# Scaled copies in three tiles, two relu groups on another engine, and a quad's work one stage later, in an attention and mixture-of-experts kernel

## The chip, the cores and the metric

The kernel runs on one core of one Trainium2 chip. The metric is the device time of one execution in microseconds; the median of the runs of a kernel is taken. The profile is one execution taken by the hardware profiler, with its own clock that begins at the first instruction; "at 162.98" means 162.98 us from there. The engines are TensorE (PE, with its weight loads PEld), VectorE (DVE), ScalarE (ACT), GpSimd (POOL) and SyncE (SP), which only issues DMAs.

## The reference

All values are fp32. A gated linear attention over batch 4, 8 heads, 768 tokens and head dimension 48 is followed by a mixture of 8 experts in which each of the 3072 tokens goes to one expert.

```python
f = 1 / (1 + exp(-f_logit))
for t in range(S):
    state = f[:, :, t, :, None] * state + einsum('bhd,bhe->bhde', k[:, :, t], v[:, :, t])
    y[:, :, t] = einsum('bhd,bhde->bhe', q[:, :, t], state)
x = y.transpose(0, 2, 1, 3).reshape(3072, 384)
logits = x @ w_gate                      # 8 experts
expert_idx = argmax(logits, 1)
gate_w = softmax(logits)[expert_idx]
for e in range(8):                       # rows of one expert
    h = maximum(x[rows_e] @ w1[e], 0)    # 384 x 1024
    out[rows_e] = gate_w * (h @ w2[e])   # 1024 x 384
```

## The kernel before

The first 140 us are the attention, in 12 units, and the routing: GpSimd scatters each token's row, with its token number and gate weight, to a table `xs` in HBM, sorted by expert. Nothing of the change touches this part.

Then the experts follow in order, 0 to 7. Each has three tiles of 128 rows (`TILES`), of which experts 0 and 1 have had their first tile done early. In experts 2 to 7 the first product (`widen_sums`, the matmuls of line 1310) is done with fewer multiplications, out of sums of the weights (`prepare_weights`, on GpSimd, line 1222, in place in the w1 tile and in `was`) and sums of the rows (`sum_rows`, on VectorE, line 1222, twelve per expert, in `xbs`). Its partial products are kept by ScalarE (line 1321) and joined by VectorE (line 1298), and ScalarE does the relu (line 1328). In experts 0 and 1 the first product is done directly (`widen`, line 387): its eight blocks of hidden units come in groups, and the relu of every other group is ScalarE's (line 397) and of the rest VectorE's (line 399).

The second product of two of the tiles is also done with fewer multiplications (`narrow_pair`, line 1360): seven products of quarter size. It needs `hidden_sums` (line 1416 and a difference), three sums of w2 (`weight_sums`, `wsum`: VectorE in experts 0 and 1, GpSimd from expert 2 on) and, in `narrow_pair` itself, two differences of the hidden units and one of w2's quarters. Four partial results are copied out of the accumulators by ScalarE, multiplied by the gate weight (`held`, line 1374); VectorE joins each with another product (`joined`, line 1378). The four copies lie in two tiles of two places each, `holdh0` and `holdh1`, handed out from the end of the list `places`: p1 and p4 in one, p5 and u2 in the other. The third tile's second product is `narrow_late` (line 403).

Rows beyond an expert's three tiles go to 8 slots of 32 rows, in two quads of four slots. A quad has its own rows (`quad_rows`: 16 small row loads and, for quad 1, four of token numbers), first weights (`quad_first`: four slots in two halves, 768 KB each, all in one tile `qw1` that both halves of both quads use in turn), second weights (`quad_second`: 1536 KB each, four buffers). `widen_quad` (line 1171) is half of a quad's first product, `turn_quad` (line 1188, "squares": `sq` in the tables) transposes its result for one slot, 32 by 32, and `turn` (`quad` in the tables) transposes its rows. Quad 0's second product rides along with the third tile of experts 4 to 7 (`narrow_riding`, line 1194); quad 1's is the last work of the kernel.

The order of the work is written out by hand. The instructions of each engine, SyncE's queue included, are issued in the order of the program. Within expert e there are three places at which loads are issued and quad products are made, numbered 3e, 3e + 1 and 3e + 2: `FIRST_AT`, `SECOND_AT`, `ROWS_AT` and `WIDE_AT` say which load or half product falls on which number. A half product falls at the start of the expert (3e) or after its `hidden_sums` (3e + 1), ahead of the loads of the same number; a load waits until the last reader of the buffer is done. `TASKS` says what VectorE does for the next expert, at four hooks of each expert: at its start, after its hidden sums, inside `narrow_pair` (`between`), and after it; `turn` transposes the next expert's rows, `sumN` makes N of its row sums. Sums not made there are made inside the next expert's `widen_sums`.

Between the first and second product of expert e the loads of expert e + 2 are issued: its rows (`load_expert`: four loads and up to three small ones), then its w1 (`load_first_weights`); its w2 (`load_second_weights`) follows the pair, since it takes the buffer of expert e's w2.

Of the kernel before, what the change touches and what calls it, by code (L numbers as in the profile page):

```python
# [11 lines left out]
F32 = mybir.dt.float32  # L12
# [37 lines left out]
SHORT = TILES * C - T  # L50
FIXED = np.array([SHORT if e in RIDE else TILES * C for e in range(E)])

ROWS_AT = {5: 0, 11: 1}
FIRST_AT = {
    4: [(0, 0, 0), (0, 1, 0)],
    7: [(0, 2, 0), (0, 3, 0)],
    9: [(0, 0, 1), (0, 1, 1)],
    10: [(0, 2, 1), (0, 3, 1)],
    13: [(1, 0, 0), (1, 1, 0)],
    14: [(1, 2, 0), (1, 3, 0)],  # L60
    16: [(1, 0, 1), (1, 1, 1)],
    17: [(1, 2, 1), (1, 3, 1)],
}
SECOND_AT = {8: [(0, 0)], 11: [(0, 1)], 14: [(0, 2)], 17: [(0, 3), (1, 0)], 19: [(1, 1)], 20: [(1, 2)]}
WIDE_AT = {9: (0, 0), 12: (0, 1), 16: (1, 0), 19: (1, 1)}


TASKS = {
    0: ("turn", "", "", ""),
    1: ("turn", "sum6", "", "sum4"),  # L70
    2: ("turn", "quad0 sum5", "sum6", "sum1"),
    3: ("turn", "sum6", "sum6", ""),
    4: ("sq00 turn", "sq01 sum3", "sum5", "sum4 quad1"),
    5: ("sq02 turn", "sq03 sum4", "sum6", "sum2"),
    6: ("turn", "sum6", "sum6", ""),
    7: ("sq10 sq11", "sq12", "sq13", ""),
}

# [93 lines left out]
def kernel(  # L172
# [205 lines left out]
    def widen(x, w, bank, blocks):  # L378

        rows = x["rows"]  # L380
        per = 512 // rows
        for b in blocks:
            i, f = divmod(b, per)
            if f == 0:
                x["h"] = bank(i)[:, 0 : per * rows].rearrange("p (f c) -> p f c", f=per)
            for j in range(KD):
                nc.tensor.matmul(  # L387
                    x["h"][:, f],
                    lhsT=w[0][:, j, b * 128 : b * 128 + 128],
                    rhs=x["xT"][:, j],  # L390
                    start=j == 0,
                    stop=j == KD - 1,
                )
            if f == per - 1:
                to = x["hT"][:, b - f : b + 1]
                if i % 2 == 0:
                    nc.scalar.activation(to, x["h"], AF.Relu)
                else:
                    nc.vector.tensor_scalar(to, x["h"], 0.0, None, op0=OP.max)
# [20 lines left out]
    HD = DM // 2  # L420
# [30 lines left out]
    def load_first_weights(e):  # L451
        w1t = wpool.tile([128, KD, F], F32, name="w1t")
        nc.sync.dma_start(w1t, moe_w1[e].rearrange(W1, p=128))
        weights[e] = [w1t]
# [6 lines left out]
    def slot(k, s, most):  # L461
        return nc.values_load(
            sloti[0:1, k, s : s + 1], [mybir.EngineType.SP], min_val=0, max_val=most
        )

    def load_expert(e):

        t = int(e < EARLY)
        x = load_rows(first[e] + t * C, int(FIXED[e]) - t * C)
        if e in RIDE:  # L470
            rows = xs[ds(slot(0, RIDE[e], NONE), T)]
            nc.sync.dma_start(x["tg"][C - T :, TILES - 1], rows[:, TOK:USED])
        return x
# [51 lines left out]
    with ExitStack() as st:  # L525
# [8 lines left out]
        for y in yt:  # L534
# [9 lines left out]
        held = {  # L544
            n: [ld.tile([128, SEG, C], F32, name=f"{n}{i}") for i in range(bufs)]
            for n, bufs in (("q", 4), ("k", 3), ("f", 2))
        }
# [581 lines left out]
    with ExitStack() as st:  # L1129
        bank, narrow_late, psz = tile_pools(st)  # L1130
        qp = st.enter_context(tc.tile_pool(name="qp", bufs=1))
# [80 lines left out]
        def minus(to, a, b, on=nc.vector):  # L1212
            on.tensor_tensor(to, a, b, op=OP.subtract)  # L1213
# [135 lines left out]
        def narrow_pair(x, s1, sums, between=lambda: None):  # L1349

            b, t1, t2, t4 = sums
            a = hidden_parts(x)
            one, two, both = (psz.tile([128, DM], F32, name="yps") for i in range(3))
            one, two, left, right = one[:, 0:HD], two[:, 0:HD], both[:, 0:HD], both[:, HD:DM]
            ysb = [ep.tile([128, DM], F32, name="ysb") for t in range(2)]
            gate = [x["tg"][:, t, 1:2] for t in range(2)]

            def product(to, h, w, start):
                for f in range(HB):
                    nc.tensor.matmul(  # L1360
                        to,
                        lhsT=h[:, f],
                        rhs=w[:, f],
                        start=start and f == 0,
                        stop=f == HB - 1,
                        skip_group_check=True,
                    )

            spare = [qp.tile([128, 2, HD], F32, name="held", tag=f"holdh{i}") for i in range(2)]
            places = [tile[:, i] for tile in spare for i in range(2)]  # L1370

            def held(part, t):
                to = places.pop()
                nc.scalar.mul(to, part, gate[t])  # L1374
                return to

            def joined(t, h, part, other):
                nc.vector.scalar_tensor_tensor(  # L1378
                    ysb[t][:, h * HD : h * HD + HD],
                    part,  # L1380
                    gate[t],
                    other,
                    op0=OP.mult,
                    op1=OP.add,
                )

            def leave(t):
                scatter(out, x["dst"][:, t : t + 1], ysb[t], N - 1, "out")

            product(one, a[0][0], b[0][0], True)  # L1390
            p1 = held(one, 0)
            minus(a[0][0], s1, a[0][0])
            product(left, a[0][1], b[1][0], True)
            minus(a[0][1], a[0][1], a[0][0])
            minus(b[0][1], b[1][1], b[0][1])
            product(right, a[1][1], t4, True)
            joined(0, 0, left, p1)
            between()
            p4 = held(right, 1)
            product(two, s1, t1, True)  # L1400
            p5 = held(two, 1)
            product(one, a[0][0], t2, False)
            u2 = held(one, 0)
            product(two, a[0][1], b[1][1], False)
            joined(0, 1, two, u2)
            leave(0)
            product(one, a[1][0], b[0][1], False)
            joined(1, 0, one, p4)
            joined(1, 1, one, p5)
            leave(1)  # L1410
# [20 lines left out]
        def fetch(at):  # L1431
            for piece in FIRST_AT.get(at, ()):
                quad_first(*piece)
            if at in ROWS_AT:
                quad_rows(ROWS_AT[at])
            for piece in SECOND_AT.get(at, ()):
                quad_second(*piece)

        for e in range(E):
            x, w = rows_of[e], weights[e]  # L1440
            end, wide = e == E - 1, e >= EARLY
# [18 lines left out]
            def wide_quad(at):  # L1460
                if at in WIDE_AT:
                    q, b = WIDE_AT[at]
                    widen_quad(quads[q], b)
# [18 lines left out]
                tasks(1)  # L1482
            wide_quad(3 * e + 1)
            if e + 2 < E:
                rows_of[e + 2] = load_expert(e + 2)
                load_first_weights(e + 2)
            fetch(3 * e + 1)
            if end:
                halves_of(quads[1], 0)
# [16 lines left out]
    with tc.If(todo > 0):  # L1506
# [80 lines left out]
        with ExitStack() as st:  # L1587
            bank, narrow_late, psz = tile_pools(st)
            hp = st.enter_context(tc.tile_pool(name="hp", bufs=1))
            with tc.For_i(0, E) as e:  # L1590
# [10 lines left out]
                with tc.For_i(e * REGION + skip, rows_to, C) as at:  # L1601
                    x = load_rows(at)
# [57 lines left out]
```

## Time and profile before

| | |
|---|---|
| median of 3 runs | 385.8 us (385.88, 385.8, 381.94) |
| the profiled execution | 381.89 us |
| its span, from the first to the last instruction | 380.0 us |
| TensorE's mean granted clock | 0.999 |
| busy: TensorE, VectorE, GpSimd, ScalarE | 361.1, 280.4, 223.1, 161.8 us |
| moved by DMA | 94.92 MB, 250 GB/s on the mean |

A row of the timeline gives the start in us, the duration, the engine ("SPq" is SyncE's queue: the time of the issue, not of the transfer), the line, the operation, the tile written and those read, and how many instructions were merged. Brackets hold the idle time of the engine just before and what ended it. A busy TensorE is not one at its peak, but an idle one does nothing.

### The profile page before, as it was taken

How to read it: one execution, taken by the hardware profiler on the slowest of the kernel's cores; microseconds unless marked ns; L12 is line 12 of the kernel's file. 1: busy time of each engine (PE TensorE's matmuls, PEld its weight loads, DVE VectorE, ACT ScalarE, POOL GpSimd, SP SyncE). 2: the span in 40 equal slices, each digit the busy share in tenths (PEclk: the TensorE clock that was granted, in tenths of full speed). 3: DMA queues.
4: the chain of work that ended last, by engine and by line, in shares of the span. 5: the costliest groups of instructions: out<-in, count | busy, mean ns of one | idle time of the engine just before them, and what ended most of it. 6: DMA issues, size and time to landing. Idle time of an engine off the chain costs nothing.

```text
span 380.0 us, 9175 instructions
## 1 busy us (share of the span) xinstructions
PE 361.1 (95%) x3438; PEld 310.5 (82%) x3438; DVE 280.4 (74%) x565; ACT 161.8 (43%) x326; POOL 223.1 (59%) x240
## 2 busy tenths in 40 slices
PE   8999999999999999998799799999998999999993
PEld 8889889888889678987797597977795599499692
DVE  6999989896974645569669848867977667878850
ACT  7899885875433001110353154245235125316410
POOL 5444255758954411069799399299579629946112
PEclk9999999999999999999999999999999999999999
DMA  7999765758994368999447699761999989981151
GB/s 261 392 384 367 255 235 201 246 197 277 401 364 134 123 178 269 288 352 299 149 152 213 218 376 262 291 218 19 258 348 383 217 329 365 373 301 41 22 187 47
DMA packets 56916, 94.92 MB, mean 250 GB/s; under 512 B 20968, under 2 KB 41003, under 8 KB 55840
## 3 DMA queue, kind: packets, MB, share of 16 engines
q1 hardware_dynamic: 53696, 84.62, 68.4%
q0 software_dynamic: 3168, 9.64, 6.7%
q8 instruction: 29, 0.48, 0.5%
q14 instruction: 23, 0.19, 0.2%
HBM read 79.23 MB, written 15.21 MB: 248 GB/s over the span
## 4 chain that ended last, share of the span: by engine, by line
PE 63%; DVE 16%; POOL 8%; issue 6%; ACT 2%; DMA 2%; SPq 1%; POOLq 0%; DVEq 0%
PE yps L1360 11%; PE hps L1310 9%; PE s L647 6%; PE yt L671 6%; PE xp L770 6%; DVE hT L1298 5%; PE yps L1194 4%; PE hps L387 4%; PE s L387 3%; POOL wsum L1213 3%; PE kp L660 3%; DVE xbs L1222 3%; PE yt L692 2%; POOL was L1222 2%; PE dp L708 2%
## 5 line engine op out<-in xcount | busy, mean ns | idle before, releaser
L246 POOL DMA_INDIRECT out_dram<-ysb,dst x26 | 26.4, 1017 | 89.0 <-DVE ysb L1378 50.7
L1360 PE MATMUL yps<-w2t,hT 128*128 128x192 f32 x256 | 45.3, 330 | 5.8 <-ACT held L1374 4.3
L1360 PEld LDWEIGHTS yps<-w2t,hT 128*128 128x128 f32 x256 | 41.6, 190 | 10.4 <-ACT held L1374 5.4
L1328 ACT ACTIVATE hT<-hT 128x352 f32<-128x352 f32 (+1 forms) x48 | 23.9, 506 | 39.1 <-DVE hT L1298 38.9
L1310 PE MATMUL hps<-xbs,w1t 128*128 128x176 f32 (+1 forms) x216 | 37.6, 318 | 0.2
L613 POOL TENSOR_TENSOR k<-k,r 128x1024 f32<-128x1024 f32 (+1 forms) x11 | 25.2, 2293 | 20.5 <-ACT r L609 14.6
L246 POOL DMA_INDIRECT xs<-xr,posi x24 | 27.3, 1135 | 16.2 <-issue 4.9
L1310 PEld LDWEIGHTS hps<-xbs,w1t 128*128 128x128 f32 x216 | 34.0, 190 | 0.7 <-issue 0.7
L1374 ACT ACTIVATE held<-yps,tg 128x192 f32<-128x192 f32 x32 | 12.4, 419 | 51.1 <-DVE ysb L1378 35.5
L653 DVE COPY_PREDICATED at<-mpack,s 128x512 f32<-128x512 uint8 x48 | 32.0, 729 | 1.9 <-PE s L647 1.9
L1321 ACT COPY hT<-hps 128x352 f32<-128x352 f32 (+1 forms) x54 | 24.8, 459 | 18.0 <-PE hps L1310 11.7
L1298 DVE TENSOR_TENSOR hT<-hps,hT 128x352 f32<-128x352 f32 (+1 forms) x42 | 22.3, 530 | 12.5 <-ACT hT L1321 5.9
L595 DVE TENSOR_TENSOR_SCAN sum<-g,cap 128x1032 f32<-128x1032 f32 (+1 forms) x14 | 29.4, 2104 | 2.1 <-ACT g L588 2.1
L1222 POOL TENSOR_TENSOR was<-w1t 128x256 f32<-128x256 f32 x30 | 26.1, 886 | 3.1 <-issue 2.6
L1194 PE MATMUL yps<-qw,hqT 128*32 128x192 f32 (+1 forms) x192 | 27.5, 381 | 0.2 <-issue 0.2
L647 PE MATMUL s<-q,k 64*128 64x128 f32 x384 | 26.8, 282 | 0.1
L1378 DVE SCALAR_TENSOR_TENSOR ysb<-yps,tg,held 128x192 f32<-128x192 f32 x32 | 12.6, 414 | 19.0 <-PE yps L1360 19.0
L647 PEld LDWEIGHTS s<-q,k 64*128 64x128 f32 x384 | 23.1, 187 | 2.9 <-issue 1.2
L770 PE MATMUL xp<-wx,ys 128*128 128x104 f32 x192 | 24.9, 279 | 0.4 <-issue 0.4
L1360 PE MATMUL yps<-wsum,hT 128*128 128x192 f32 x128 | 23.6, 327 | 1.2 <-DVE hT L1213 1.2
L671 PE MATMUL yt<-at,v 128*48 128x128 f32 x384 | 24.6, 276 | 0.1
L770 PEld LDWEIGHTS xp<-wx,ys 128*128 128x128 f32 x192 | 22.9, 192 | 1.2 <-issue 0.9
(157 smaller groups left out, 836.7 us busy)
## 6 DMA issues: line engine op xcount, KB each, us to landing
w1t<-in_moe_w_dram SPq DMA_DIRECT2D x8, 1536.0 KB
w2t<-in_moe_w_dram SPq DMA_DIRECT2D x8, 1536.0 KB, 12.5
qw<-in_moe_w_dram SPq DMA_DIRECT2D x16, 768.0 KB, 8.8
qw<-in_moe_w_dram SPq DMA_DIRECT2D x8, 1536.0 KB
k<-in_ku_dram SPq DMA_DIRECT2D x12, 512.0 KB
q<-in_qu_dram SPq DMA_DIRECT2D x12, 512.0 KB, 6.8
f<-in_fu_dram SPq DMA_DIRECT2D x10, 512.0 KB, 5.6
xs<-pad SPq DMA_DIRECT2D x8, 600.0 KB
```

Of the source, the lines that this page charges most:

```text
L246: ins = nc.gpsimd.indirect_dma_start(out=dst, out_offset=bass.IndirectOffsetOnAxis(ap=idx, axis=0), in_=src, in_offset=None, bounds_check= ...
L387: nc.tensor.matmul(x["h"][:, f], lhsT=w[0][:, j, b * 128 : b * 128 + 128], rhs=x["xT"][:, j], start=j == 0, stop=j == KD - 1,)
L595: nc.vector.tensor_tensor_scan(x["sum"][:, part].rearrange("p s c -> p (s c)"), x["g"][:, part].rearrange("p s c -> p (s c)"), cap[:, part ...
L647: done["score"] = nc.tensor.matmul(ps[h][:, p], lhsT=x["k"][r, s], rhs=x["q"][r, s], start=True, stop=True).ins
L653: nc.vector.copy_predicated(x["at"][:, a, h], _bc(causal, 1, HP), x["ps", a][h])
L671: nc.tensor.matmul(x["yt"][a][DP * (h ^ a) : DP * (h ^ a) + D, p], lhsT=x["v"][:, a, 2 * p + h], rhs=x["at"][:, a, h, p], start=p == 0, st ...
L770: nc.tensor.matmul(x["xp", a][:, p], lhsT=x["ys", a][:, p], rhs=wx[:, p, 0:XW] if a else wx[:, p, E:WX], start=True, stop=True,)
L1194: nc.tensor.matmul(yp[r], lhsT=h[:, f, at : at + T], rhs=w[:, f, cols], start=f == order[0], stop=f == order[-1], skip_group_check=True,)
L1222: on.tensor_tensor(to, first[1], second[1], op=op)
L1298: nc.vector.tensor_tensor(place(to), one, place(other), op=op)
L1310: nc.tensor.matmul(banks[n][:, g], lhsT=lhs[:, C * g : C * g + C], rhs=rhs, start=op == "new" and g == 0, stop=True, skip_group_check=True,)
L1360: nc.tensor.matmul(to, lhsT=h[:, f], rhs=w[:, f], start=start and f == 0, stop=f == HB - 1, skip_group_check=True,)
```

## The change

1. The four scaled copies of `narrow_pair` lie in three tiles: p1 in the first, p4 and u2 in the second, p5 in the third. The first join is issued ahead of the difference of w2's quarters instead of behind it.
2. In experts 0 and 1 all four relu groups are ScalarE's (`x["wide"]` is False there; the tiles done early have no such entry and stay as they were).
3. In expert 0 the w1 of expert 2 is loaded ahead of its rows instead of behind them. The other experts keep their order.
4. Quad 1 goes one stage on: its rows are loaded in expert 4 (14) instead of expert 3 (11), its first weights from 13 to 19 instead of 13 to 17, its half products are made at 19 and 21 instead of 16 and 19. Quad 0's second weights 3 are loaded at 16 instead of 17, quad 1's 1 at 17 instead of 19. Two of the squares and the turn of quad 1 go one hook or more on, and row sums move with them.

```diff
-ROWS_AT = {5: 0, 11: 1}
+ROWS_AT = {5: 0, 14: 1}
 FIRST_AT = {
...
-    13: [(1, 0, 0), (1, 1, 0)],
-    14: [(1, 2, 0), (1, 3, 0)],
-    16: [(1, 0, 1), (1, 1, 1)],
-    17: [(1, 2, 1), (1, 3, 1)],
+    13: [(1, 0, 0)],
+    14: [(1, 1, 0)],
+    16: [(1, 2, 0), (1, 3, 0)],
+    19: [(1, 0, 1), (1, 1, 1), (1, 2, 1), (1, 3, 1)],
 }
-SECOND_AT = {8: [(0, 0)], 11: [(0, 1)], 14: [(0, 2)], 17: [(0, 3), (1, 0)], 19: [(1, 1)], 20: [(1, 2)]}
-WIDE_AT = {9: (0, 0), 12: (0, 1), 16: (1, 0), 19: (1, 1)}
+SECOND_AT = {8: [(0, 0)], 11: [(0, 1)], 14: [(0, 2)], 16: [(0, 3)], 17: [(1, 0), (1, 1)], 20: [(1, 2)]}
+WIDE_AT = {9: (0, 0), 12: (0, 1), 19: (1, 0), 21: (1, 1)}
...
 TASKS = {
     0: ("turn", "", "", ""),
-    1: ("turn", "sum6", "", "sum4"),
-    2: ("turn", "quad0 sum5", "sum6", "sum1"),
+    1: ("turn", "sum6", "", "sum3"),
+    2: ("turn", "quad0 sum3", "sum6", "sum3"),
     3: ("turn", "sum6", "sum6", ""),
-    4: ("sq00 turn", "sq01 sum3", "sum5", "sum4 quad1"),
-    5: ("sq02 turn", "sq03 sum4", "sum6", "sum2"),
-    6: ("turn", "sum6", "sum6", ""),
+    4: ("sq00 turn", "sq01 sum3", "sum5", "sum4"),
+    5: ("turn", "sq02 sum3", "sum6 quad1", "sum3"),
+    6: ("turn", "sq03 sum3", "sum6", "sum3"),
     7: ("sq10 sq11", "sq12", "sq13", ""),
 }
...
-                if i % 2 == 0:
+                if i % 2 == 0 or x.get("wide") is False:
                     nc.scalar.activation(to, x["h"], AF.Relu)
                 else:
                     nc.vector.tensor_scalar(to, x["h"], 0.0, None, op0=OP.max)
...
-            spare = [qp.tile([128, 2, HD], F32, name="held", tag=f"holdh{i}") for i in range(2)]
-            places = [tile[:, i] for tile in spare for i in range(2)]
+            spare = [qp.tile([128, 2, HD], F32, name="held", tag=f"holdh{i}") for i in range(3)]
+            places = [spare[i][:, j] for i, j in ((1, 1), (2, 0), (1, 0), (0, 0))]
...
             minus(a[0][1], a[0][1], a[0][0])
-            minus(b[0][1], b[1][1], b[0][1])
             product(right, a[1][1], t4, True)
             joined(0, 0, left, p1)
+            minus(b[0][1], b[1][1], b[0][1])
             between()
...
             if e + 2 < E:
+                if e == 0:
+                    load_first_weights(e + 2)
                 rows_of[e + 2] = load_expert(e + 2)
-                load_first_weights(e + 2)
+                if e > 0:
+                    load_first_weights(e + 2)
```

## The prediction

> **What bounds the kernel now.** I read the page first, then TensorE in order of time from 143 us on (the only stretch that the change touches), then the idle times that end there, then the stretches of the DMA queue and the issues of SyncE's queue.
>
> ```profile
> span 380.0 us, 9175 instructions
> PE 361.1 (95%) x3438; PEld 310.5 (82%) x3438; DVE 280.4 (74%) x565; ACT 161.8 (43%) x326; POOL 223.1 (59%) x240
> ```
>
> TensorE is busy for 361.1 of 380.0 us, so everything that an edit without a matmul can bring lies in some 19 us of holes. No matmul is added or removed. The holes of the expert stage, by the timeline of TensorE (start, duration, engine, line, operation, tiles, count, and in brackets the idle time before it and what ended it):
>
> ```profile
> 176.10 0.92 PE L1360 MATMUL yps<-w2t,hT 128*128 128x192 f32 x4 [1.51 <-DVE hT L399]
> ...
> 183.21 2.87 PE L1360 MATMUL yps<-w2t,hT 128*128 128x192 f32 x16 [1.99 <-ACT held L1374]
> ...
> 210.87 1.54 PE L1360 MATMUL yps<-wsum,hT 128*128 128x192 f32 x8 [1.16 <-DVE hT L1213]
> 213.54 2.87 PE L1360 MATMUL yps<-w2t,hT 128*128 128x192 f32 x16 [1.13 <-ACT held L1374]
> ...
> 244.23 2.87 PE L1360 MATMUL yps<-w2t,hT 128*128 128x192 f32 x16 [0.25 <-ACT held L1374]
> ...
> 249.74 0.86 PE L1310 MATMUL hps<-xT,was 128*128 128x176 f32 x4
> ...
> 274.82 2.87 PE L1360 MATMUL yps<-w2t,hT 128*128 128x192 f32 x16 [0.88 <-ACT held L1374]
> 277.52 0.76 PE L1310 MATMUL hps<-xT,was 128*128 128x176 f32 x4
> ...
> 294.76 2.33 PE L1171 MATMUL hps<-qw,qxT 128*32 128x512 f32 x17 [1.03 <-DMA qw<-in_moe_w_dram]
> ...
> 311.82 0.76 PE L1310 MATMUL hps<-xT,was 128*128 128x176 f32 x4
> ...
> 324.13 2.78 PE L1171 MATMUL hps<-qw,qxT 128*32 128x512 f32 x24
> ...
> 341.21 0.76 PE L1310 MATMUL hps<-xT,was 128*128 128x176 f32 x4
> ```
>
> Experts 5, 6 and 7 begin at 277.52, 311.82 and 341.21. Expert 5 is the slow one: 34.3 us, with a quad's first product (L1171) in it that waits for its weights. Behind the `held` rows stands one line of the waits (engine and line, what it waited for, us in total, times, longest):
>
> ```profile
> ACT held L1374 <- DVE ysb L1378: 35.5, 8, 8.0
> ```
>
> In all 8 experts a scaled copy waits for a join on VectorE. The second copy p4 lies in the tile that holds p1, which the join reads: a write behind a read. The joins queue behind w2's sum.
>
> **The change, part by part.** Expert 1 first. VectorE's rows, then GpSimd's, SyncE's, a group of ScalarE, and two stretches of the DMA queue (busy times of the engines, clock, DMA share, GB/s):
>
> ```profile
> 162.98 1.76 DVE L370 STREAM_TRANSPOSE xT<-xrow 128x1152 f32<-128x1152 f32 x1
> ...
> 167.50 0.69 DVE L399 TENSOR_SCALAR hT<-hps 128x512 f32<-128x512 f32 x1 [2.71 <-PE hps L387]
> ...
> 176.15 1.11 DVE L1416 TENSOR_TENSOR hsum<-hT 128x512 f32<-128x512 f32 x1
> ...
> 178.50 1.03 DVE L1213 TENSOR_TENSOR hT<-hsum,hT 128x512 f32<-128x512 f32 x1
> ...
> 180.59 1.48 DVE L1213 TENSOR_TENSOR w2t<-w2t 128x768 f32<-128x768 f32 x1
> ```
> ```profile
> 166.90 0.72 POOL L1222 TENSOR_TENSOR was<-w1t 128x256 f32<-128x256 f32 x1 [2.59 <-issue]
> ...
> 183.29 0.72 POOL L1222 TENSOR_TENSOR w1t<-w1t,was 128x256 f32<-128x256 f32 x1
> ```
> ```profile
> 154.15 3.21 SPq L340 DMA_DIRECT2D xrow<-xs  x4
> ...
> 157.97 0.43 SPq L453 DMA_DIRECT2D w1t<-in_moe_w_dram  x1
> ```
> ```profile
> L397 ACT ACTIVATE hT<-hps 128x512 f32<-128x512 f32 x4 | 2.4, 599 | 23.9 <-PE hps L387 13.8 <-DMA xrow<-xs 10.1
> ```
> ```profile
> 157.00:161.00 4.00, 4.00 (x27) 4.00 (x26) 1.23 (x3) 1.15 (x3) 0.00 (x0) 1.00 1.26 232
> 161.00:164.50 3.50, 3.50 (x20) 3.22 (x20) 2.60 (x4) 0.00 (x0) 1.94 (x2) 1.00 1.00 397
> ```
>
> The relus: four of 0.69 us leave VectorE and cost ScalarE four of 0.60 us; ScalarE was idle for 23.9 us ahead of that group, which hides them. The 1.51 us hole goes. Late next is the hidden sum, which stands in VectorE's order behind the turn of expert 2's rows, w2's three sums and six row sums. Here the swap of the loads counts. The rows fill the queue over 157 to 161 us and w1 over 161 to 164.5; w1 ahead (1536 KB at 397 GB/s, 4.0 us) puts the rows' end at about 165. The turn began at 162.98, some 2 us behind the rows' end, so it goes to about 167, 4 us later. VectorE had 2.71 us of idle time and two relus (1.4 us) there, which the change frees, so the hidden sum starts at 176, as before. Bounds of the swap: 0 (the turn waits less than I think) to 4 us (all of it comes through). GpSimd's sums of expert 2's first weights can start some 2.5 us sooner than 166.90 and end at 181.5 instead of 184.0; without the swap they would end 0.4 us behind the start of expert 2 found below, so at this place the swap only keeps GpSimd off the path. On TensorE: `left` ends at 175.2 instead of 176.8, the product of s1 starts at 177.2, that of s1 minus a00 at 179.5 (as before: hsum, two differences of about 1.1 us). From there p4 and p5 no longer wait for a join: the 1.99 us go, but the last product needs w2's sum, which now runs behind the join, 181.0 to 182.5. Expert 2 starts at 183.6 instead of 185.9: **2.3 us** (1 to 3).
>
> Expert 2: two of five row sums move behind the pair.
>
> ```profile
> 208.22 1.57 DVE L1222 TENSOR_TENSOR xbs<-xT,xbs 128x192 f32<-128x192 f32 x2
> 209.71 0.41 DVE L1222 TENSOR_TENSOR xbs<-xbs,xT 128x192 f32<-128x192 f32 x1
> ```
>
> Half of 1.57 and 0.41 make 1.2 us, so the 1.16 hole closes, and 1.13 with the tiles: **2.2 us**. The sums are issued after the pair, in front of expert 3's turn, where VectorE has slack. Experts 3 and 4: **0.25 and 0.88**. Together TensorE reaches expert 5 about 5.6 us earlier, at **271.9**.
>
> Expert 5 loses the quad's first half (L1171, 2.7 us as at 324.13), the second quad's turn and one set of squares. What is left has the shape of expert 4 without its hole: 277.52 - 249.74 - 0.88 = 26.9 us. Expert 6 gets the first half in the place of the second; expert 7 gets the second half ahead of everything, 2.7 us more. The squares are VectorE's transposes:
>
> ```profile
> L1188 DVE STREAM_TRANSPOSE hqT<-hq 32x256 f32<-32x256 f32 x32 | 13.9, 436 | 3.1 <-ACT hq L1179 2.6
> ```
>
> A set is four of 436 ns, 1.7 us. Expert 6 gets one in exchange for three of six row sums, less than 1 us more ahead of its pair (bounds 0 and 1 us; I take 0). In expert 7 two sets, 3.5 us, must wait for the second half's product and relu; the joins behind them start about as long after the first matmul of the expert's own as before, since that comes 2.7 us later too (bounds 0 and 2 us, taken as 0). If no load is late, expert 6 starts at 298.8, expert 7 at 328.1, and the end is 328.1 + 2.7 + (380.0 - 341.2) = **369.6**.
>
> **The loads.** The second half's four loads now wait for the first half's product in expert 6 (one buffer), and stand behind w2 of expert 7 and three loads of second weights. Can the queue bring them by 328.1? Stretches of the queue, then SyncE's issues, then the traffic of its hardware queue from 312 to 341 us, and of all issues those of a quad's rows (two quads, KB each, us to landing):
>
> ```profile
> 247.00:266.00 19.00, 19.00 (x157) 14.33 (x160) 13.72 (x24) 9.21 (x21) 17.76 (x18) 1.00 0.42 118
> ...
> 312.00:340.00 28.00, 27.95 (x217) 22.38 (x217) 23.47 (x40) 11.43 (x26) 22.36 (x23) 1.00 1.02 356
> ```
> ```profile
> 247.17 0.40 SPq L458 DMA_DIRECT2D w2t<-in_moe_w_dram  x1
> ...
> 264.23 0.39 SPq L1149 DMA_DIRECT2D qw<-in_moe_w_dram  x1
> ...
> 273.44 0.35 SPq L453 DMA_DIRECT2D w1t<-in_moe_w_dram  x1
> ...
> 278.07 0.40 SPq L458 DMA_DIRECT2D w2t<-in_moe_w_dram  x1
> ...
> 301.28 0.35 SPq L453 DMA_DIRECT2D w1t<-in_moe_w_dram  x1
> ...
> 312.06 0.40 SPq L458 DMA_DIRECT2D w2t<-in_moe_w_dram  x1
> ```
> ```profile
> q1 hardware_dynamic: 6003, 9.44, 92.9%
> ```
> ```profile
> qrow<-xs SPq DMA_DIRECT2D x32, 12.0 KB, 1.9
> ```
>
> From 247.17 to 264.23 SyncE issues one w2 and then the quad's 20 small row loads, and the DMA engines are busy for 0.42 of it: 17 us in which the queue runs dry. The change moves that block behind w2 of expert 6, whose issue waits for expert 4's last product (278.07, 0.55 us behind 277.52). The chain from there: 271.9 + 0.55 for w2; 17.1 for the block and 2.3 more for the 768 KB load now ahead of it (0.79 MB at 28 us per 9.44 MB), so the third second-weight load is issued at 291.9; 9.2 to w1 of expert 7 (264.23 to 273.44, the same sequence), 301.1; 10.8 for w1 and two first-half loads (301.28 to 312.06, the same kinds), 311.9, which is about when expert 6's quad product wants them (298.8 + 12.1). Then w2, three second weights and the four loads: 4 x 1.573 + 4 x 0.786 MB = 9.44 MB, which is what the queue moved from 312 to 340 in before: 28 us. So they are in at 339.9; with 1 us of slack at either seam closed up, at 337.9. I take **338.9**. TensorE stands from 328.1 to 338.9, and the end is 338.9 + 2.7 + 38.8 = **380.4**. What was gained is handed back at the start of expert 7.
>
> On the rule: the Trainium skill, DMA: Bandwidth & Descriptors, section Issuing engines are not separate DMA queues, says that the sequencer's issue time is usually small relative to the DMA itself. Here 16 issues of 12 KB and four smaller ones take most of 17 us for 0.2 MB, and the trace disagrees. By that rule the block would cost its bytes alone, about 0.6 us, the chain would be some 15 us shorter, and the end would be that of the rival without a late load.
>
> **The rivals.**
>
> Nothing late: span 369.6. The loads must be in 11 us sooner than my chain has it. It holds if SyncE's block of small loads runs faster in its new place, or if the transfers behind it overlap more than one after the other. For it: the queue had room in before (0.42 over 247 to 266). Against it: the same bytes stood in the queue at a share of 1.02. Each us that my chain is too long is a us gained, so the cases between (373 to 377) belong here.
>
> Slower, through expert 1's queue on VectorE: if the turn of expert 2's rows ends not at 168.8 but 4 us later, w2's sums, the row sums and the hidden sum follow it in order, expert 2 starts at 187.6, and since the chain hangs on expert 4's end, everything is 4 us later: 384.4. It decides from a turn that begins later than 170.9. For it: the queue is full there (shares of 1.26 and 1.00), so w1 delays the rows by its whole length; against: that length is only 4.0 us, and VectorE's idle time takes up most of it.
>
> The change does not do what it says: p4's wait is for the shared accumulator of `left` and `right`, not for the tile. Then the four `held` holes stay (4.25 us); about 1 us of each goes with the earlier join, so 2 us come back, and the chain ends at 382.5.
>
> **How the numbers follow.** 1% (3.8 us) is about what a measurement of this kernel can tell. Forecast 0.48, with 377 to 384; nothing or little late 0.33 (369 to 377); slower through VectorE 0.14; not as said 0.05. The profiled execution took 381.89 us, 1.9 beyond its span; the timed runs were 385.88, 385.8 and 381.94, two levels 3.9 apart, and the profile is on the lower. My span 380.4 makes 382.3 on the lower level and 386.2 on the upper; I cannot say on which the next median falls and put down 384. The range goes from a mostly kept gain on the lower level (371.5 to 373) to 384.4 + 1.9 + 3.9 less a little: 373 to 389. The gains over 1% are 0.35 (nothing late and a small part of the forecast), slower 0.16.
>
> **What would show it.** The relu's 1.51 us and the `held` rows of 1.99, 1.13 and 0.88 gone; expert 5 starting near 272 and taking about 27 us; SyncE's small row loads now between about 275 and 291; four 768 KB loads issued near 315; and, decisive, an idle time of some 11 us on TensorE ahead of L1171 at the start of expert 7, ended by the DMA of `qw`. I am wrong if that idle time is under 5 us, or if the turn at expert 1 begins past 171.

## The result and the profile after

The changed kernel takes 386.69 us (median of 20 runs, 382.92 to 389.05), the kernel before 382.76 us in the same comparison (20 runs, 379.02 to 385.92). The ratio is 1.0107, with a 95% interval of 1.0077 to 1.0138: **1% slower**. The forecast was no change (a span of 380.4 us against 380.0). The profiled execution after has a span of 384.9 us, 4.9 more than before, so the traces show the difference with the same sign and about the same size.

The page of the changed kernel, its first lines:

```profile
span 384.9 us, 9171 instructions
PE 364.3 (95%) x3438; PEld 308.9 (80%) x3438; DVE 279.4 (73%) x561; ACT 164.3 (43%) x330; POOL 220.7 (57%) x240
```

TensorE has the same 3438 matmuls and is busy 3.2 us longer. That alone says that not all of the loss is waiting; some matmuls ran slower or alone. TensorE's timeline from expert 1 on (start, duration, line, tiles, count, and in brackets the idle time before it and what ended it):

```profile
178.47 1.57 PE L1360 MATMUL yps<-wsum,hsum 128*128 128x192 f32 x8 [2.24 <-DVE hsum L1416]
180.83 1.54 PE L1360 MATMUL yps<-wsum,hT 128*128 128x192 f32 x8 [0.79 <-DVE hT L1213]
182.63 2.87 PE L1360 MATMUL yps<-w2t,hT 128*128 128x192 f32 x16 [0.26 <-ACT held L1374]
185.33 0.81 PE L1310 MATMUL hps<-xT,was 128*128 128x192 f32 x4
...
195.74 1.54 PE L1310 MATMUL hps<-xbs,w1t 128*128 128x192 f32 x8 [0.50 <-DVE xbs L1222]
203.61 1.56 PE L403 MATMUL yps<-w2t,hT 128*128 128x384 f32 x4 [0.43 <-ACT hT L1328]
...
275.19 0.76 PE L1310 MATMUL hps<-xT,was 128*128 128x176 f32 x4
...
303.34 0.76 PE L1310 MATMUL hps<-xT,was 128*128 128x176 f32 x4
...
335.13 1.05 PE L1171 MATMUL hps<-qw,qxT 128*32 128x512 f32 x2 [0.94 <-DMA qw<-in_moe_w_dram]
337.17 1.05 PE L1171 MATMUL hps<-qw,qxT 128*32 128x512 f32 x2 [0.99 <-DMA qw<-in_moe_w_dram]
339.62 1.04 PE L1171 MATMUL hps<-qw,qxT 128*32 128x512 f32 x2 [1.41 <-DMA qw<-in_moe_w_dram]
342.10 4.10 PE L1171 MATMUL hps<-qw,qxT 128*32 128x512 f32 x18 [1.43 <-DMA qw<-in_moe_w_dram]
346.13 0.86 PE L1310 MATMUL hps<-xT,was 128*128 128x176 f32 x4
```

Read from the bottom. At the start of expert 7 four rows in a row wait for `qw`, the four loads of quad 1's second half. From 335.13 to 346.13 TensorE does 24 matmuls that took 2.78 us in expert 6 of before: 8.2 us lost. Expert 5 begins at 275.19, 2.3 us sooner than before (277.52), expert 6 at 303.34, 8.5 us sooner; 2.7 of these are the quad product that is only postponed to expert 7, so 5.8 were gained. Expert 6 up to its last product takes 31.8 us instead of 29.4 (303.34 to 335.13, with the first 0.94 of the wait; 311.82 to 341.21), and 5.8 - 2.4 - 8.2 makes 4.8 of the 4.9 us lost (the rest is rounding). In expert 1, the two old holes (1.51 and 1.99) have become three new ones (2.24, 0.79, 0.26): 3.50 us out, 3.29 us in.

SyncE's queue and the stretches of the DMA engines behind it (for the stretches: busy times of the engines, then granted TensorE clock, DMA share, GB/s):

```profile
275.43 0.39 SPq L458 DMA_DIRECT2D w2t<-in_moe_w_dram  x1
...
277.96 1.90 SPq L340 DMA_DIRECT2D qrow<-xs  x4
...
294.56 0.39 SPq L1149 DMA_DIRECT2D qw<-in_moe_w_dram  x1
...
302.25 0.35 SPq L453 DMA_DIRECT2D w1t<-in_moe_w_dram  x1
```
```profile
283.00:295.00 12.00, 11.96 (x106) 8.20 (x105) 10.21 (x16) 5.44 (x12) 11.52 (x15) 1.00 0.22 62
295.00:312.00 17.00, 15.55 (x97) 14.59 (x95) 14.59 (x30) 5.10 (x13) 10.46 (x10) 1.00 1.00 307
312.00:344.00 32.00, 26.86 (x190) 17.01 (x194) 19.47 (x38) 7.38 (x17) 23.04 (x24) 0.96 1.06 381
```

The rows of the quad stand between 277.96 and 294.56. From 283 to 295 the DMA engines are at a share of 0.22. Then they are full, 1.00 and 1.06, until the last late load is in. What they could have moved in those 12 us is missing at 335; e4 below tests this.

### The profile page after: what moved, and what is told of

The parts are those of the page before. It is cut to its first block, busy times and chain, and to the rows that moved or that the text cites. A ratio compares the mean times of both kernels' runs of the same rounds, so it can differ in the third digit from the quotient of the medians.

```text
span 384.9 us, 9171 instructions
## 1 busy us (share of the span) xinstructions
PE 364.3 (95%) x3438; PEld 308.9 (80%) x3438; DVE 279.4 (73%) x561; ACT 164.3 (43%) x330; POOL 220.7 (57%) x240
## 4 chain that ended last, share of the span: by engine, by line
PE 61%; DVE 18%; DMA 8%; SPq 5%; issue 3%; ACT 3%; POOL 1%; POOLq 0%; DVEq 0%
PE hps L1310 11%; PE yps L1360 8%; PE s L647 6%; PE yt L671 6%; DVE hT L1298 6%; PE xp L770 6%; PE yps L1194 4%; DMA qw<-in_moe_w_dram 4%; SPq L1149 3%; PE s L387 3%; DVE xbs L1222 3%; PE hps L387 3%; PE kp L660 3%; DMA xrow<-xs 3%; PE hps L1171 2%
## 5 line engine op out<-in xcount | busy, mean ns | idle before, releaser
L595 DVE TENSOR_TENSOR_SCAN sum<-g,cap 128x1032 f32<-128x1032 f32 (+1 forms) x14 | 29.3, 2102 | 2.0 <-ACT g L588 1.9
L1188 DVE STREAM_TRANSPOSE hqT<-hq 32x256 f32<-32x256 f32 x32 | 14.0, 436 | 14.2 <-ACT hq L1179 13.8
L1378 DVE SCALAR_TENSOR_TENSOR ysb<-yps,tg,held 128x192 f32<-128x192 f32 x32 | 12.6, 414 | 15.8 <-PE yps L1360 12.2
L1222 POOL TENSOR_TENSOR was<-w1t 128x256 f32<-128x256 f32 x30 | 23.2, 790 | 1.1 <-PE hps L387 0.6
```

The costliest lines, as they stand in the source:

```text
L595: nc.vector.tensor_tensor_scan(x["sum"][:, part].rearrange("p s c -> p (s c)"), x["g"][:, part].rearrange("p s c -> p (s c)"), cap[:, part ...
L1222: on.tensor_tensor(to, first[1], second[1], op=op)
```

## The experiments

Time is given as a ratio to the kernel before on the same chip, with its 95% interval. The three chips of the experiments ran the kernel before in 378.9 to 379.2 us, 1% faster than the chip of the result, so spans are best compared by stages. The last column counts, in each trace, from the first matmul of expert 1's pair to the first matmul of expert 7's own product (172.48 to 341.21 in before). What follows it takes 38.8 us in before and after alike, and 37.7 to 38.0 us in all experiments. A stage is read from one execution of a kernel, and the gain over before by the stage and by the timed ratio differ by up to 1.9 us either way; differences of a few tenths between two stages say where something moved, not what a kernel is worth.

| kernel | time, us | ratio to before | stage, us |
|---|---|---|---|
| before | 378.9 to 379.2 here, 382.76 in the result | 1 | 168.7 |
| the change | 386.69 | 1.0107 (1.0077 to 1.0138) | 174.0 |
| e1 quad as before | 374.88 | 0.9885 (0.9835 to 0.9934) | 166.1 |
| e2 quad alone | 386.24 | 1.0183 (1.0137 to 1.0229) | 174.9 |
| e3 halves ahead | 373.71 | 0.9846 (0.9798 to 0.9894) | 164.1 |
| e4 rows back | 373.28 | 0.9870 (0.9817 to 0.9924) | 163.3 |
| e5 e4 and swap undone | 371.72 | 0.9811 (0.9761 to 0.9862) | 161.4 |
| e6 e4 and two tiles | 374.01 | 0.9844 (0.9790 to 0.9898) | 164.5 |
| e7 e4 and accumulators apart | 374.87 | 0.9875 (0.9824 to 0.9927) | 163.7 |
| e8 e4 and four sums | 373.84 | 0.9836 (0.9789 to 0.9882) | 164.4 |
| e9 e3, e4 and swap undone | 372.80 | 0.9835 (0.9789 to 0.9880) | 161.2 |
| e10 e9 and four sums | 370.61 | 0.9775 (0.9738 to 0.9812) | 161.7 |
| e11 quad mended, alone | 377.87 | 0.9981 (0.9957 to 1.0005) | 166.6 |
| e12 one load behind | 375.84 | 0.9902 (0.9867 to 0.9938) | 166.7 |

**Is it the quad, or the rest?** e1 takes the quad's five tables (`ROWS_AT`, `FIRST_AT`, `SECOND_AT`, `WIDE_AT`, `TASKS` 4 to 6) from before into the changed kernel; e2 takes them from the change into the kernel before.

```diff
-ROWS_AT = {5: 0, 14: 1}
+ROWS_AT = {5: 0, 11: 1}
...
-WIDE_AT = {9: (0, 0), 12: (0, 1), 19: (1, 0), 21: (1, 1)}
+WIDE_AT = {9: (0, 0), 12: (0, 1), 16: (1, 0), 19: (1, 1)}
```

> The changed kernel with the second quad where the kernel before has it (its rows, loads and squares go back one stage; three tiles, join order, relus and the turned-round loads stay). Theory of the queue (the loss lies in the moved quad alone, at the start of expert 7): expert 5 starts near 275.2, as in the changed kernel, keeps the 34.3 us of before, and the end is 380.0 - 2.3 = 377.7, 0.6% faster than before; no idle time over 3 us ahead of L1171 after 300 us. Rival (the new order of copies, relus and loads in experts 1 to 4 costs in all later experts): span 384 or more, as in the changed kernel.

> The kernel before with the second quad alone moved one stage on, as the change has it. Theory of the queue: expert 5 starts at 277.5 as before, the four loads of the second half land 66.9 us later, at 344.4, TensorE stands some 7 to 8 us ahead of L1171 at the start of expert 7, and the end is 344.4 + 2.7 + 38.8 + the slow clock's 1.3 = 387.2, 1.9% slower than before. Rival (the moved quad is neutral, the loss comes from the rest): span 380 or less.

e1 is 1.15% faster than before (0.7 to 1.7%, more than the 0.6% expected), e2 is 1.8% slower. In e1 the stage is 2.7 us shorter than before, near the 2.3 expected. e2 keeps every hole of before in experts 1 to 4 and has the late loads:

```profile
182.19 2.87 PE L1360 MATMUL yps<-w2t,hT 128*128 128x192 f32 x16 [1.99 <-ACT held L1374]
...
276.49 0.76 PE L1310 MATMUL hps<-xT,was 128*128 128x176 f32 x4
```
```profile
342.19 4.46 PE L1171 MATMUL hps<-qw,qxT 128*32 128x512 f32 x18 [2.10 <-DMA qw<-in_moe_w_dram]
346.58 0.86 PE L1310 MATMUL hps<-xT,was 128*128 128x176 f32 x4
```

From expert 5's start to the end of the wait it is 342.19 - 276.49 = 65.7 us, against 66.9 in the changed kernel and 66.9 expected. So the loss is the moved quad's, whole, and the other parts are a gain. The rival, a cost in the new order of copies, relus and loads, has fallen.

**What makes the loads late.** e3 sends the four loads ahead of two second weights of 1.5 MB. e12 sends them ahead of one. e4 takes the rows alone back to 11.

```diff
 # e3
-SECOND_AT = {..., 16: [(0, 3)], 17: [(1, 0), (1, 1)], 20: [(1, 2)]}
+SECOND_AT = {..., 16: [(0, 3)], 20: [(1, 0), (1, 1), (1, 2)]}
 # e12
+SECOND_AT = {..., 16: [(0, 3)], 17: [(1, 0)], 20: [(1, 1), (1, 2)]}
 # e4
-ROWS_AT = {5: 0, 14: 1}
+ROWS_AT = {5: 0, 11: 1}
```

> The changed kernel with the four loads of the quad's second half (768 KB each, 3.1 MB in all) issued ahead of the second weights (1,0) and (1,1) instead of behind them. Theory of the queue (the loads are late by the bytes that stand ahead of them): two loads of 1.57 MB less ahead, 3.15 MB at 381 GB/s, 8.3 us sooner; they land at 333.8, TensorE is ready for them at 335.1, so the stall falls from 11 us in all to 3 us or less, and the end is 376 to 377. Rival (they are late because their buffer comes free late, with the first half's product at 317 to 319, and for the 3.1 MB themselves): they gain 3 us at most, end 382 to 385.

> The changed kernel with the 20 small loads of the second quad's rows issued one stage sooner, ahead of w2 of expert 6 as in the kernel before; all weights of the quad stay where the change has them. Theory of the queue run dry (from 283 to 295 us the DMA engines are at a share of 0.22 while SyncE issues the rows): the loads behind it start some 9 to 15 us sooner, the second half lands before TensorE wants it (by 335), no stall over 3 us at the start of expert 7, end 375 to 377. Rival (the bytes or the buffers of the last stages set it, not the row loads): end 384.9 as in the changed kernel, within 1.5 us.

> The changed kernel with one of the two loads of 1.57 MB, (1,1), behind the four loads of the second half, and (1,0) still ahead of them: half the dose of e3. In the changed kernel the last of the four loads ended TensorE's wait 6.97 us behind the first product of expert 7 (335.13 to 342.1), and the 18 matmuls behind the wait took 4.10 us at a granted clock of 0.57. Theory of the queue: 1.57 MB at 381 GB/s is 4.1 us, so the wait ends 2.9 us behind the first product; from the first product to the expert's own first matmul it takes 4.9 us if the clock stays at 1.00, 6.9 us if a wait of this length slows it too, against 11.0 us in the changed kernel and 2.7 without a wait; end 4 to 6 us sooner than the changed kernel, 0 to 0.7% faster than before. Rival (the place of the loads in the queue has a threshold, all or nothing): 2.7 or 11 us.

TensorE at the start of expert 7, first in e3, then in e4, then in e12:

```profile
331.51 2.78 PE L1171 MATMUL hps<-qw,qxT 128*32 128x512 f32 x24
334.23 0.86 PE L1310 MATMUL hps<-xT,was 128*128 128x176 f32 x4
```
```profile
330.83 2.80 PE L1171 MATMUL hps<-qw,qxT 128*32 128x512 f32 x24
```
```profile
330.94 1.81 PE L1171 MATMUL hps<-qw,qxT 128*32 128x512 f32 x6
333.76 2.76 PE L1171 MATMUL hps<-qw,qxT 128*32 128x512 f32 x18 [1.01 <-DMA qw<-in_moe_w_dram]
336.45 0.86 PE L1310 MATMUL hps<-xT,was 128*128 128x176 f32 x4
```

In e3 and e4 the 24 matmuls are one row again, with no wait in it. In e12, half the dose, the wait ends 333.76 - 330.94 = 2.8 us behind the first product: 2.9 was expected from 1.57 MB at 381 GB/s, and the changed kernel has 7.0. No, half and whole dose give 7.0, 2.8 and none. That is a queue and not a threshold. (I had the 18 matmuls behind the wait at 2.0 us; at full clock they take 2.7, so it is 5.5 us from first product to own matmul, not 4.9.)

Why a mere 0.2 MB of rows decide is seen in two stretches of e4:

```profile
247.00:266.00 19.00, 19.00 (x155) 15.48 (x155) 16.18 (x27) 9.35 (x21) 18.28 (x20) 1.00 0.48 154
...
283.00:292.00 9.00, 9.00 (x89) 5.48 (x88) 7.29 (x11) 4.17 (x10) 8.68 (x12) 1.00 1.14 294
```

The rows run the queue dry here too, 0.48 from 247 to 266. But nothing that is wanted soon stands behind them there: TensorE does not stand for a load in experts 4 and 5. From 283 to 292 the queue is full, where the changed kernel had 0.22. Expert 7's w1 is issued at 292.18 instead of 302.25, and the whole tail behind it follows.

**What the pieces in experts 1 to 6 are worth.** All four are on top of e4, where no load hides their effect. No run undoes the relus or the order of the first join alone, so how the gain of e1 divides between these two is not shown. e5 takes the turned-round loads of expert 0 back; e6 the third tile; e7 puts `right` beside `one`; e8 gives expert 1 its fourth row sum again.

```diff
 # e5
-                if e == 0:
-                    load_first_weights(e + 2)
                 rows_of[e + 2] = load_expert(e + 2)
-                if e > 0:
-                    load_first_weights(e + 2)
+                load_first_weights(e + 2)
 # e6: spare in range(2), places as before the change
 # e7
-            one, two, left, right = one[:, 0:HD], two[:, 0:HD], both[:, 0:HD], both[:, HD:DM]
+            one, right, two, left = one[:, 0:HD], one[:, HD:DM], two[:, 0:HD], both[:, 0:HD]
 # e8
-    1: ("turn", "sum6", "", "sum3"),
+    1: ("turn", "sum6", "", "sum4"),
```

> From here on with the second quad's rows back in their old place, so that no load is late. In expert 0 the loads go out again with the rows of expert 2 ahead of its first weights. Theory (VectorE's queue in expert 1 is held up by the wait for the rows, 4.0 us in the kernel with the rows back): the turn begins some 4 us sooner, the hidden sum comes 2 to 3 us sooner, the two idle times of 1.70 and 0.79 us in expert 1's pair close, and the pair takes 10.2 to 10.8 us on TensorE instead of 12.6; end 2 us sooner than with the rows back alone, 0.5% more gain. Rival (GpSimd's sums of expert 2's first weights, which start later without the turned-round loads, hold expert 2 instead): the same end within 0.5 us, with a wait for w1t or was in expert 2.

> The rows back, and the scaled copies in two tiles, as before the change. Theory (the copy p4 waits for the join because left and right share one accumulator tile; the third tile takes no wait away): every stage of experts 1 to 6 within 0.3 us of the kernel with the rows back, the wait of held for a join on VectorE there 8 times as with three tiles. Rival (the tile that p4 shares with p1 makes it wait): the waits grow, 0.3 to 1 us more in each pair of experts 1 to 6, end 2 to 4 us later.

> The rows back, and the product called right accumulates in the free half of the tile of the product called one instead of beside left. Theory (the shared accumulator makes p4 wait): the 8 waits of held for a join are gone, so are TensorE's idle times ahead of the last product of a pair (0.26 in expert 1, 0.24 in 3, 0.26 in 5), and the end is 0.5 to 1 us sooner. Rival (the wait is for the tile of copies, or for the order on VectorE): the 8 waits stay, and the end with them.

> The rows back, and four row sums instead of three at the end of expert 1 (as before the change; expert 2 keeps its three at each place). Theory (the row sum moved into expert 2 is what TensorE waits for there, 0.49 us ended by VectorE's xbs): that idle time goes, expert 2's wide part takes 13.0 us instead of 13.8, end 0.5 to 0.8 us sooner. Rival (the sum only moves the wait): end unchanged within 0.3 us.

*e5.* VectorE in expert 1, first with the rows back, then with the swap undone as well:

```profile
164.89 1.79 DVE L370 STREAM_TRANSPOSE xT<-xrow 128x1152 f32<-128x1152 f32 x1 [4.02 <-DMA xrow<-xs]
...
174.79 1.21 DVE L1416 TENSOR_TENSOR hsum<-hT 128x512 f32<-128x512 f32 x1
```
```profile
161.45 1.76 DVE L370 STREAM_TRANSPOSE xT<-xrow 128x1152 f32<-128x1152 f32 x1
...
171.78 0.69 DVE L1416 TENSOR_TENSOR hsum<-hT 128x512 f32<-128x512 f32 x1 [0.47 <-ACT hT L397]
```

The 4.02 us of waiting for rows are gone, and with them every hole of the pair: it takes 180.04 - 170.94 = 9.1 us on TensorE instead of 12.6. So the swap costs 3.5 us in expert 1. GpSimd's last sum of expert 2's first weights ends at 180.6 and holds nobody, since expert 2 begins at 180.04 and goes on without a wait for it: what the swap was to prevent did not come. Of the 3.5 us, 1.9 are left in the stage; expert 2 now waits 0.97 for a row sum and expert 6 1.02 us for a join. The timed gain over e4 is 0.6%, and the two intervals overlap.

*e6.* Two tiles or three: experts 2 to 6 agree within 0.3 us, and the line of the waits has the same 8 waits as with three (31.8, 8, 7.2 in e4). The pair of expert 1 is 0.8 us longer, but not by the tiles: the product of s1 waits 2.34 us for the hidden sum instead of 1.70, since the rows came later (4.28 us of waiting for 4.02), and behind that wait the clock fell (last section). The time of e6 is the same within the intervals. *e7* has `right` in another accumulator tile. By the size of its error, its result lacks the first product of `one` (last section); all instructions and waits are in it. The two lines of the waits for the copies, e6 above and e7 below:

```profile
ACT held L1374 <- DVE ysb L1378: 32.0, 8, 7.5
```
```profile
ACT held L1374 <- PE yps L1360: 39.6, 30, 2.8
```

With the accumulators apart not one copy waits for a join any more. So p4 waited for the join because `left` and `right` share an accumulator that both engines read, and not because p1 and p4 shared a tile of copies. Four pairs (experts 1, 3, 4 and 5) are 0.3 to 0.6 us shorter than in e4, 1.9 together, and expert 2's pair is 0.4 shorter too, but the quad product behind that takes 2.0 us longer, with the first quad's loads late in it ([0.99 <-DMA qw] ahead of L1171 at 214.73). The stage is 0.4 us longer than e4's and the time within its interval: the 0.5 to 1 us expected did not come. The 1.99, 1.13 and 0.88 holes of before stay closed in e6, without the third tile; what else could close them is the join, which is issued ahead of w2's sum in both (not tested alone).

*e8.* Expert 2 waits no longer for a row sum (its part up to the pair takes 18.4 us instead of 19.7), but its pair is 0.9 longer: 0.3 us are left. And the quad's 24 matmuls at the start of expert 7 take 1.6 us longer in this trace, with a wait for `qw` in them: in e4 the last of the four loads landed at 330.83, just as TensorE reached it.

**Put together.** e9 is e3, e4 and e5 in one; e10 adds e8's sum. e11 puts the mended quad (e3 and e4) into the kernel before, with none of the rest.

> The rows back in their old place, the four loads of the second half ahead of (1,0) and (1,1), and the turned-round loads of expert 0 undone. Theory (with the rows back alone the last of the four loads landed at 330.82, when TensorE reached them at 330.83; there is no room, and bytes ahead of them are what sets it): they land 4 us or more ahead of TensorE, no idle time over 0.3 us ahead of L1171, (1,0) and (1,1) still come before TensorE wants them near 346; end as with the swap undone or up to 1 us sooner, 2.0 to 2.3% faster than before. Rival (the second weights are now late): an idle time ahead of L1194 in expert 7 of 2 us or more, and the end 2 us later.

> The kernel of e9 with four row sums instead of three at the end of expert 1. With the swap undone, expert 2 waited 0.97 us for a row sum (xbs). Theory: that idle time goes, expert 2 up to its pair takes 18.4 us instead of 20.1, and 0.5 to 1 us of it comes back in expert 2's pair, as it did in e8; end 0.5 to 1.2 us sooner than e9. Rival (all of it comes back in the pair): the end within 0.3 us of e9.

> The kernel before with the second quad's products and squares one stage on, as the change has it, but its rows in their old place and the four loads ahead of (1,0) and (1,1); nothing else of the change. Theory (the moved quad is worth something once no load is late: experts 5 to 7 up to the start of the last wide part took 61.1 us with the rows back against 63.7 before): no idle time over 1 us ahead of L1171, end 2 to 3.5 us sooner than before, 0.5 to 0.9% faster. Rival (the gain of the kernels with the rows back is all of the other parts): the time of before within 0.3%.

The lowest time is e10's, 370.61 us, 2.25% faster than before (1.9 to 2.6%). By stages e9 and e10 are alike (161.2 and 161.7): in e10's trace the sum gives 1.2 us in expert 2 up to its pair, and the pair takes 0.9 more and the quad product behind it 1.2 more, with this row:

```profile
209.64 3.97 PE L1171 MATMUL hps<-qw,qxT 128*32 128x512 f32 x24
```

Quad 0's first half takes 3.97 us instead of 2.78, since its fourth load ends a wait in it (at 210.85). In e9 TensorE comes to this product at 210.34, and the fourth load, issued at 201.24, landed 8.2 us later, at 209.4. In e10 TensorE comes 0.7 us sooner, but that alone would not have made it wait: the load, issued at 201.37, took 9.4 us to land. Why it took longer is not shown. The intervals of e5, e9 and e10 overlap, and I do not call e10 better than e9. In e9 the last of the four loads lands at 329.33 and TensorE reaches them at 330.00: 0.7 us of room, not the 4 expected, since they can be issued only when the first half's product has read their buffer (315.67). The second weights behind them hold nobody; that rival has fallen. e11's stage is 2.1 us shorter than before's, its timed gain is 0.19% with an interval that includes none. That the mended quad is worth something by itself is therefore open; the other parts of the change together are worth 1.15% without it (e1).

## Why the prediction was wrong

**The mechanism of the late loads was right.** It named the place (L1171 at the start of expert 7), the cause (`qw`'s second half, late by way of the rows' block in SyncE's queue) and the chain: from expert 5's start to the loads in 67.0 us predicted (271.9 to 338.9), 66.9 measured (275.19 to 342.10). e2, e3, e4 and e12 each moved one link of it and got what it says. The length of the wait was not right: TensorE was to stand for 10.8 us, from 328.1 on. It came to the product at 334.19, 6.1 us later than forecast (3.3 by expert 5's start, the rest since experts 5 and 6 took 28.2 and 30.9 us and not 26.9 and 29.3), and got past the wait at 342.10, 7.9 us later; 4.8 us of these are idle in the four rows and the rest lies in the short products between them. By the prediction's own sign, an idle time under 5 us, the idle rows alone would have counted as wrong.

**What it hangs on was mis-sized.** The end is the sum of three terms. Predicted: 338.9 + 2.7 + 38.8 = 380.4. Measured: 342.1 + 4.0 + 38.8 = 384.9.

1. *Expert 5's start, 3.3 us late (275.19 for 271.9).* The gains ahead of it were 2.3 us and not 5.6. Of the 2.3, 0.3 us stood already at the start of expert 1's pair (172.17 for 172.48).
 - Expert 1: 2.3 predicted, 0.3 by the length of its stretch. The failed step is the swap, which I priced at nothing because the hidden sum would come at 176 "as before". That price compares with before, and not with the change without the swap: the time that the relus freed on VectorE was spent on a wait of 4.20 us for the rows. Without the swap (e5) the hidden sum starts at 171.78, and its pair has no hole. The 3.5 us of e5 lie just below the upper bound of 4 that I gave the swap and did not take. Nor did the sum come at 176. The turn came as predicted (167; measured 166.95), the hidden sum at 177.21, since the six row sums ahead of it took 5.0 us (1.67, 1.57, 0.88, 0.87) and not 3.6 (1.68, 1.23, 0.35, 0.34). So the products of s1 and of s1 minus a00, forecast at 177.2 and 179.5, came at 178.47 and 180.83. The row sums are as long in e5 (0.88, 0.87), so that is not the swap's doing; why they are longer than before no run tests.
 - Expert 2: 2.2 predicted, 1.2 measured. The pair gained 2.4; but the part up to it lost 1.2, of which 0.50 in front of 195.74 and 0.43 in front of 203.61. I counted the two sums moved behind expert 2's pair and overlooked the one that left expert 1's end. e8 shows it.
 - Experts 3 and 4: 0.25 and 0.88 predicted, -0.3 and 0.9 measured.
2. *The product behind the wait, 4.0 us instead of 2.7.* The sum took it at full clock, without a reason; the granted clock was 0.50 (last section).
3. The rest of expert 7, 38.8 in both.

So the forecast failed by 3.3 us of gains that were not there and 1.3 us of a slower clock, and those two, less 0.1 by which the chain was shorter, are all of the 4.5 us.

**The rivals.** *Nothing late* was wrong for this kernel, and in e3 and e4, where nothing is late, the stages are 4.6 and 5.5 us shorter than before: about half of the 10.4 us that this rival promised. Of the 4.9 us that e4 lacks, 2.7 lie in experts 1 to 4 and 2.2 in experts 5 and 6, which took 28.2 and 30.2 us and not 26.9 and 29.3. *Slower, through VectorE's queue of expert 1* gave 384.4 and the trace has 384.9, but by chance: its condition, a turn that begins later than 170.9, did not occur; the row sums, expert 2 and the clock made up the sum. *The change does not do what it says* had the right reason for p4's wait, the shared accumulator, and e7 shows it. I gave it 0.05, though nothing in the profile before spoke for the tile: the waits name the join that is waited for, not what is shared with it. The holes it was to leave closed all the same, so its 382.5 was wrong.

**What was to show it.** Seen: the relu hole and the 1.99, 1.13 and 0.88 gone (0.26 left), the rows at 278 to 294, and an idle time behind `qw`, shorter than forecast. Not seen: expert 5 near 272; it took 28.2 us and not 27, with 0.58 and 0.26 of it waits in its pair. The four loads were issued at 320 to 328 and not near 315: their buffer came free with expert 6's quad product, which ended at 319.7 (316.95 + 2.78), since expert 6 began at 303.34 and not at 298.8. The queue was full either way, so they landed when the bytes ahead of them were through.

## What to carry to other kernels

A load is late by what stands ahead of it, and what stands ahead is time as well as bytes: 20 issues of 12 KB and less, 0.2 MB in all, took 16.6 us of the queue (277.96 to 294.56). So ask of every block of small loads whether the queue can afford to run dry at its place. A gain on an engine is only counted once the next thing behind it has been sized anew, and against the kernel that has the gain: a sum that comes "as before" has already spent what was freed ahead of it. And a schedule without slack can lose a gain at the next load: the waits for quad 0's loads in e7 and e10 and for quad 1's in e8 stand where e4 and e9 had 0.0 to 0.9 us of room.

## What the runs showed of the hardware

**The clock fell behind a wait.** In the changed kernel TensorE's granted clock, by stretches of 1 us (the number before the last two):

```profile
340.00:341.00 1.00, 0.67 (x2) 0.00 (x0) 0.00 (x0) 0.00 (x0) 0.92 (x2) 1.00 0.99 377
341.00:342.00 1.00, 0.00 (x0) 0.00 (x0) 0.00 (x0) 0.00 (x0) 0.92 (x1) 0.71 1.08 382
342.00:343.00 1.00, 0.90 (x8) 0.24 (x12) 0.00 (x0) 0.00 (x0) 0.00 (x0) 0.50 1.05 369
343.00:344.00 1.00, 1.00 (x12) 0.34 (x8) 0.00 (x0) 0.00 (x0) 0.00 (x0) 0.50 1.05 357
344.00:345.00 1.00, 1.00 (x12) 0.18 (x2) 0.00 (x0) 0.00 (x0) 0.00 (x0) 0.58 0.14 49
345.00:346.00 1.00, 1.00 (x6) 0.11 (x1) 0.00 (x0) 0.00 (x0) 0.00 (x0) 1.00 0.04 15
```

After 7 us with three short products in them, the clock is at 0.50 for about 3.4 us, just when the loads have come: 18 matmuls take 4.1 us instead of 2.76. e2, which waited as long, shows the same (0.50, and 4.46 us). e12, where the wait ended 2.8 us behind the first product, keeps 1.00 and 2.76. So in these two kernels the long wait cost its length and 1.3 to 1.7 us more. But a long wait is not needed. e6 shows the same drop in expert 1, its row first and then the clock by stretches of 1 us:

```profile
176.72 2.74 PE L1360 MATMUL yps<-wsum,hsum 128*128 128x192 f32 x8 [2.34 <-DVE hsum L1416]
```
```profile
176.00:177.00 1.00, 0.28 (x1) 0.28 (x2) 0.97 (x2) 0.00 (x0) 1.00 (x2) 0.98 0.89 354
177.00:178.00 1.00, 1.00 (x5) 1.00 (x5) 0.90 (x2) 0.00 (x0) 0.25 (x1) 0.50 1.03 397
180.00:181.00 1.00, 1.00 (x7) 1.00 (x6) 0.58 (x1) 0.48 (x2) 0.00 (x0) 0.82 0.70 260
```

There 2.34 us without a matmul were enough, while the changed kernel keeps 1.00 behind its 2.24 us at the same place (178.47). What decides between the two no run tests. The Trainium skill, TensorE: Matmul & The Clock Gate, Part 1, says that the clock is halved after an idle window of about 3.4 us and comes back after as long a busy one. The 3.4 us at half clock agree. An idle window of 3.4 us does not: the longest idle time around the drop was 1.43 us in the changed kernel, 2.10 in e2 and 2.34 in e6, so less than a full window without a matmul was enough here.

**The start of a product resets its neighbour.** e7's `right` began in the other half of the tile in which `one` was still open, and the output is off by a relative 0.504, which fits that `one` lost what it had. My estimate for a first product that is missing in three of the four quarters of two tiles in three, with all quarter products of one size, is the root of 3/8 x 2/3, 0.50. The Trainium skill, PSUM — Partial Sum Buffer, The four PSUM rules, says so of two accumulation groups in one bank; the run agrees.

**Two engines that read the same accumulator tile do so one after the other in this program:** the copy waits for the join though neither writes it, 8 times in every kernel but e7, where `left` and `right` lie apart (the two lines of the waits above).
